# Attention in six whole-kind bundles per pass, and TensorE's queue in source order, from unit 5 on

## The chip, the cores and the metric

The kernel runs on one core of a Trainium2 chip. The metric is device time in microseconds, lower is better: the median of several executions of the whole program. Five engines work side by side, each through its own queue in order: TensorE (PE; its weight loads are listed apart as PEld), VectorE (DVE), ScalarE (ACT), GpSimd (POOL) and SyncE (SP), which here issues nearly all DMA transfers.

## The reference

The program is a gated linear attention with complex decay, followed by a bilinear feed-forward, all in float32.

```python
B, H, S, D = 4, 8, 768, 48
mag = sqrt(a_re**2 + a_im**2); scale = min(mag, 0.999) / (mag + 1e-6)
for t in range(S):                       # state S_re, S_im: [B, H, D, D]
    new_re = ar * S_re - ai * S_im       # ar, ai: the scaled decay of step t
    new_im = ar * S_im + ai * S_re
    S_re, S_im = new_re + outer(k[t], v[t]), new_im
    y[t] = q[t] @ S_re
x = y as [3072, 384]
out = ((x @ w_a) * (x @ w_b)) @ w_out    # w_a, w_b: [384, 1536], w_out: [1536, 384]
```

## The kernel before, in words

The recurrence is computed in chunks of 128 time steps, the feed-forward for 256 tokens at a time. The unit of work is one chunk of two batch rows, called halves i = 0 and 1 here: 6 chunks times 2 pairs make NU = 12 units of 256 tokens. Units 0 to 5 are the six chunks of the first pair, 6 to 11 those of the second, so units 0 and 6 are first chunks (no state comes in) and units 5 and 11 last ones (no state goes out).

A unit goes through three stages.

*Preparation* (`prep` and `scale`, VectorE and ScalarE): running products of the complex decay over the chunk, and their product with q and k, into the tile `qk`. Ten DMA transfers on SyncE's queue (`stack`) then lay `qk` out anew as `stk`, one column block for each head. `qk` and `stk` exist once each: the transfers wait until TensorE has read the old `stk`, and the next `qk` load stands behind them in the queue.

*Attention* (`attn`, mostly TensorE), for each half i: **scores** (8 matmuls, two PSUM tiles "pm" of four heads; VectorE masks each into a tile "am"), **transposes** of the scaled k (8, into two "pm" tiles; ScalarE copies them to "kt"), **outputs** (masked scores times v plus, except in a first chunk, the incoming state times q, in four column tiles of the array, into "xp"; ScalarE copies this to "xh" and VectorE puts the rounding residual, the piece **residual**, into "xl"), and **state** (8 matmuls into two "pm" tiles; VectorE adds them to the state tile "u"). Scores, transposes and state are given out in two groups hg of four heads, outputs in two halves. Full float32 matmuls appear as two records each in the profile. The pool of "pm" has two buffers, "am" and "kt" have two each, "xp" has one.

*Feed-forward* (`gemm1` and `gemm2`): a pass over twelve blocks f0 to f11 of the hidden dimension. The first GEMM of a block is 18 matmuls into "ab" (hi and lo parts of x and the weights, so that a fast float format reaches float32 accuracy); ScalarE and VectorE form the product of the two halves and split it into "hh" and "hl"; the second GEMM, 6 matmuls, follows LAG = 2 blocks later.

The main loop runs pass w of the feed-forward on unit w, and inside it the attention of unit w + 1 and the preparation of units w + 2 and w + 3. What is given out where is written in that loop: `attn` is a generator that issues one piece at each step, and `slot()` takes steps from it, twice in each block, from block ATTN_AT = 6 on; at block STACK_AT = 10 it is drained. So in passes 4 and later, block f6 has its pieces one after the first GEMM and one after the second. These orders are only proposals: a list scheduler builds the queue of each engine from priorities (source order, brought forward for instructions inside `tc.high_priority`) and from its own estimate of when operands are ready. It does so once, when the program is built; on the chip each queue then runs in that fixed order.

The order of attention pieces before, for all units but the first, is the list `order`:

```python
order = [(scores, 0, 0), (scores, 0, 1), (transposes, 0, 0), (transposes, 0, 1),
         (outputs, 0, 0), (outputs, 0, 1), (scores, 1, 0), (residual, 0, 0), (state, 0, 0), (scores, 1, 1),
         (state, 0, 1), (transposes, 1, 0), (transposes, 1, 1), (outputs, 1, 0),
         (outputs, 1, 1), (state, 1, 0), (residual, 1, 0), (state, 1, 1)]
```

Lines that are named later: scores L385, mask L388, transposes L396, their copy L400, outputs L425, copy to xh L429, residual L434, state L442, its addition L449, first GEMM L486, its product and split L494 to L497, second GEMM L504, qk load L340, stack L352; in the preparation L292, L297, L300, L306, L322 to L328.

Of the kernel before, what the change touches and what calls it, by code (L numbers as in the profile page):

```python
# [20 lines left out]
NCH = S // C  # L21
# [25 lines left out]
EARLY = 2  # L47
WARM = 8
HB = 3
O_BUFS = 3  # L50
CONV_ON_AB = 7
NCHK = NU * G + NU + 1
# [6 lines left out]
STACK_AT = (11, 11, 11, 10, 10)  # L59
# [11 lines left out]
def tile_kernel(ctx: ExitStack, tc: tile.TileContext, a_d, qk_d, v_d, w_d, qn_d, kn_d, vn_d, an_d, out_d):  # L71
    nc = tc.nc
    vec, act, pe, sync = nc.vector, nc.scalar, nc.tensor, nc.sync
# [57 lines left out]
    def split_weights():  # L131
        for f in range(NF):
            for m, (c0, n) in enumerate(WPART):
                raw = raws[f, m]
                t = moe.tile([128, n], F32, name="o_sb", bufs=O_BUFS)
                tu = t.bitcast(U32)
# [202 lines left out]
    def load_qk(u):  # L339
        sync.dma_start(out=qk[:, :, 1, 0:2 * TOK], in_=qk_d[u])  # L340

    def stack(u, cols=None):
        n = RUN if rescaled(u % NCH) else 2 * TOK
        if cols is None:
            cols = slice(TOK if u < EARLY else 0, n)
        for h in range(H):
            r0 = h * D
            while r0 < (h + 1) * D:
                j, p = divmod(r0, 128)
                m = min((h + 1) * D - r0, 128 - p)  # L350
                d0 = 2 * (r0 - h * D)
                sync.dma_start(out=stk[d0:d0 + 2 * m, h, cols], in_=qk[p:p + m, j, :, cols])  # L352
                r0 += m
# [4 lines left out]
    def load_v(u):  # L358
        for i in range(2):
            t = vpool.tile([128, 512], F32, name="v_t")  # L360
            sync.dma_start(out=t, in_=v_d[u, i])
            v_tiles[u, i] = t
# [8 lines left out]
    def attn(u, xh, xl):  # L371

        c = u % NCH
        last = c + 1 == NCH
# [61 lines left out]
        def state(i, hg):  # L436
# [10 lines left out]
            with tc.high_priority(offset=ATTN_FIRST):  # L447
# [4 lines left out]
                if rescaled(c):  # L452
                    vec.tensor_tensor(out=uv, in0=uv, in1=sv, op=ALU.mult)
# [5 lines that stand above are left out]
        if u == 0:  # L459
            order = [(scores, 0, 0), (scores, 0, 1), (outputs, 0, 0), (outputs, 0, 1), (scores, 1, 0), (scores, 1, 1),  # L460
                     (residual, 0, 0), (outputs, 1, 0), (outputs, 1, 1), (transposes, 0, 0), (transposes, 0, 1),
                     (residual, 1, 0), (state, 0, 0), (state, 0, 1), (transposes, 1, 0), (transposes, 1, 1),
                     (state, 1, 0), (state, 1, 1)]
        for fn, i, g in order:
            if not (last and fn in (transposes, state)):
                fn(i, g)
                yield

    def pieces(u):
        return 12 if u % NCH + 1 == NCH else 18  # L470

    def new_x():
        return (moe.tile([128, NJ, TOK], F32, name="xh"), moe.tile([128, NJ, TOK], F32, name="xl"))
# [6 lines left out]
    def gemm1(f, xh, xl, ps_ab=ps_ab, moe=moe):  # L480
        ab = ps_ab.tile([128, 512], F32, name="ab")
        for m in range(2):
            n = 0
            for i in range(NJ):
                for part, xt in ((0, xh), (0, xl), (1, xh)):
                    pe.matmul(out=ab[:, m * TOK:(m + 1) * TOK],  # L486
                              lhsT=r(w_ab(f, part, m * NJ + i)),
                              rhs=r(xt[:, i, :]), start=n == 0, stop=n == 8)
                    n += 1
        h_t = moe.tile([128, TOK], F32, name="h_t")  # L490
        hh = moe.tile([128, TOK], F32, name="hh", bufs=HB)
        hl = moe.tile([128, TOK], F32, name="hl", bufs=HB)
        with tc.high_priority(offset=MOE_FIRST):
            act.copy(out=h_t, in_=ab[:, 0:TOK])  # L494
            vec.tensor_tensor(out=h_t, in0=ab[:, TOK:2 * TOK], in1=h_t, op=ALU.mult)  # L495
            act.copy(out=r(hh), in_=h_t)  # L496
            vec.tensor_tensor(out=r(hl), in0=h_t, in1=hh, op=ALU.subtract)  # L497
        return hh, hl

    def gemm2(f, hh, hl, os_):  # L500
        for tt in range(2):
            ts = slice(tt * 128, (tt + 1) * 128)
            for n, (ht, part) in enumerate(((hh, 0), (hh, 1), (hl, 0))):
                pe.matmul(out=os_[tt][:, 0:DM], lhsT=r(ht[:, ts]), rhs=r(w_t[f, 2][:, part, :]),  # L504
                          start=(f == 0 and n == 0), stop=(f == NF - 1 and n == 2))
# [107 lines left out]
    def drain(gen, ns=None):  # L613
        if gen is None:
            return
        left = ns
        for cost in gen:
            if left is not None:
                left -= cost or 0
                if left <= 0:  # L620
                    return
# [10 lines left out]
    for _ in attn(0, *x_cur):  # L632
        drain(p1, P1_A)
    pend = []

    def second():
        w2, f2, hh, hl, os2 = pend.pop(0)
        gemm2(f2, hh, hl, os2)
        if f2 == NF - 1:
            for tt in range(2):  # L640
                o_sb = moe.tile([128, DM], F32, name="o_sb", bufs=O_BUFS)
                with tc.high_priority(offset=MOE_FIRST):
                    act.copy(out=o_sb, in_=os2[tt][:, 0:DM])
                act.dma_start(out=out_d[w2, tt], in_=o_sb)

    pgen = None
    for w in range(NU):
        last = w + 1 == NU
        x_nxt = None if last else new_x()
        at = None if last else attn(w + 1, *x_nxt)  # L650
        if not last:
            load_v(w + 1)
        os_ = [ps_o.tile([128, 512], F32, name=f"o{t}") for t in range(2)]
        slots = [0, 2 * (STACK_AT[min(w, 4)] + 1 - max(ATTN_AT[min(w, 4)], 0 if w else P1_AT + 1))]
        left = [pieces(w + 1)]

        def slot():
            if at is None or f < ATTN_AT[min(w, 4)] or (w == 0 and f <= P1_AT) or not slots[1]:
                return
            n = -(-left[0] // slots[1])  # L660
            slots[1] -= 1
            for _ in range(n):
                next(at, None)
                left[0] -= 1

        for f in range(NF):
            if w == 0:
                next(ws, None)
                drain(p1, P1_F)
                if f == P1_AT:  # L670
                    drain(p1)
                    stack(1)
                    for i in range(WARM):
                        wp = ps_m.tile([128, 512], F32, name="pm")
                        pe.matmul(out=wp[:, 0:TOK], lhsT=ident, rhs=qk[:, i % NJ, 1 - i // NJ % 2, TOK:2 * TOK],
                                  start=True, stop=True)
                    load_qk(2)
                    pgen = prep(2)
            pend.append((w, f, *gemm1(f, *x_cur), os_))
            slot()  # L680
            if len(pend) > LAG:
                second()
            slot()
            if f == STACK_AT[min(w, 4)]:
                drain(at)
                if w + 2 < NU:
                    drain(pgen)
                    stack(w + 2)
                if w + 3 < NU:
                    load_qk(w + 3)  # L690
                    pgen = prep(w + 3)
            if w > 0:
                drain(pgen, 2400)
        x_cur = x_nxt
# [8 lines left out]
    vec.tensor_scalar(out=bad, in0=tot[0:1, 0:1], scalar1=128.0 * NCHK, scalar2=None, op0=ALU.not_equal)  # L703
    while pend:
        second()
    fast.close()
    with tc.If(nc.values_load(bad[0:1, 0:1], min_val=0, max_val=1) > 0):
        token_by_token()
# [55 lines left out]
```

## Time and profile before

| | |
|---|---|
| median of 3 runs | 699.11 us (698.85 to 699.16) |
| the profiled execution | 698.89 us, span 697.2 us |
| TensorE busy | 655.2 us, 94% |
| its weight loads | 610.8 us, 88% |
| VectorE busy | 551.8 us, 79% |
| ScalarE busy | 308.9 us, 44% |

Busy time is the union of an engine's instructions. Matmuls overlap in the array and their ends are modelled, so the time that a group of matmuls costs TensorE is read from its start to the start of the next group. A line of the timeline has start, length, engine, source line, operation, output and inputs, shape and count, and in brackets how long the engine stood idle just before and what ended that. A row of the table of stretches has the stretch, its length, the busy time and the number of instructions of PE, PEld, DVE, ACT and POOL, the granted clock of TensorE, the share of DMA time and the DMA rate.

### The profile page before, as it was taken

What the parts mean: (1) busy time and instruction counts of PE and PEld (TensorE: products, weight loads), DVE (VectorE), ACT (ScalarE), POOL (GpSimd) and SP (SyncE); (2) the same over time, 40 slices, a digit from 0 to 9 for tenths busy, and PEclk for the clock granted to TensorE, in tenths of its full rate; (3) what the DMA queues carried; (4) which work ended last, traced back from release to release, by engine and by line L of the source; (5) the groups of instructions that cost most, each with busy time, mean ns of one, the idle gap of its engine ahead of it and who ended that gap; (6) DMA issues with size and microseconds to landing.
All of it is one profiled execution on the core that took longest, in us unless ns stands there. A gap on an engine that the chain in (4) does not pass through costs nothing.

```text
span 697.2 us, 14316 instructions
## 1 busy us (share of the span) xinstructions
PE 655.2 (94%) x5854; PEld 610.8 (88%) x5854; DVE 551.8 (79%) x1241; ACT 308.9 (44%) x618; POOL 5.6 (1%) x11
## 2 busy tenths in 40 slices
PE   3557999999999999999999999999999999999996
PEld 1224889899899999999999999999999999999996
DVE  5999899988888889989899898999989853232221
ACT  6357755634535445245363554535542332221221
POOL 3000000000000000000000000000000000000000
PEclk9567999999999999999999999999999999999999
DMA  8973202411414205134151340511510500400000
GB/s 312 402 291 108 79 1 54 129 55 55 128 42 130 81 28 149 60 98 129 25 160 46 102 134 1 169 67 47 145 46 2 165 25 17 106 24 2 24 1 28
DMA packets 32088, 63.94 MB, mean 92 GB/s; under 512 B 3984, under 2 KB 10640, under 8 KB 32016
## 3 DMA queue, kind: packets, MB, share of 16 engines
q1 hardware_dynamic: 28560, 58.23, 27.0%
q10 hardware_dynamic: 3456, 4.72, 1.9%
q8 instruction: 48, 0.79, 0.5%
q14 instruction: 24, 0.20, 0.1%
HBM read 39.32 MB, written 4.72 MB: 63 GB/s over the span
## 4 chain that ended last, share of the span: by engine, by line
PE 64%; DVE 27%; ACT 4%; DMA 2%; issue 1%; SPq 1%; ACTq 0%; DVEq 0%
PE ab L486 30%; PE o L504 14%; PE xp L425 6%; PE pm L385 5%; PE pm L442 4%; DVE a_t L292 3%; DVE pr L230 2%; DVE qk L312 2%; DVE h_t L495 2%; PE pm L396 2%; DVE hl L497 2%; PE pm L150 2%; DVE z L297 2%; DVE pb L260 1%; DVE z L236 1%
## 5 line engine op out<-in xcount | busy, mean ns | idle before, releaser
L486 PE MATMUL ab<-xh,w 128*128 128x256 f32 x1728 | 339.0, 285 | 0.0
L486 PEld LDWEIGHTS ab<-xh,w 128*128 128x128 f32 x1728 | 278.1, 190 | 1.8 <-issue 1.4
L486 PE MATMUL ab<-xl,w 128*128 128x256 f32 x864 | 245.1, 284 | 0.0
L486 PEld LDWEIGHTS ab<-xl,w 128*128 128x128 f32 x864 | 164.4, 190 | 0.5 <-issue 0.2
L504 PE MATMUL o<-w,hh 128*128 128x384 f32 x576 | 152.3, 344 | 0.0
L494 ACT COPY h_t<-ab 128x256 f32<-128x256 f32 x144 | 53.1, 369 | 176.9 <-PE ab L486 176.8
L495 DVE TENSOR_TENSOR h_t<-ab,h_t 128x256 f32<-128x256 f32 x144 | 60.5, 420 | 72.5 <-ACT h_t L494 72.3
L504 PEld LDWEIGHTS o<-w,hh 128*128 128x128 f32 x576 | 96.8, 190 | 3.7 <-issue 3.0
L504 PE MATMUL o<-w,hl 128*128 128x384 f32 x288 | 96.9, 336 | 0.0
L496 ACT CAST hh<-h_t 128x256 fp32r<-128x256 f32 x144 | 58.0, 403 | 81.1 <-DVE h_t L495 80.9
L497 DVE TENSOR_TENSOR hl<-h_t,hh 128x256 fp32r<-128x256 f32 x144 | 60.5, 420 | 17.5 <-ACT hh L496 17.3
L150 PE MATMUL ab<-o_sb,ident 128*128 128x384 f32 x42 | 29.1, 794 | 29.9 <-DVE o_sb L141 29.8
L385 PE MATMUL pm<-stk 128*128 128x128 f32 x384 | 54.4, 279 | 2.7 <-DMA stk<-qk 2.7
L504 PEld LDWEIGHTS o<-w,hl 128*128 128x128 f32 x288 | 54.1, 188 | 0.0
L385 PEld LDWEIGHTS pm<-stk 128*128 128x128 f32 x384 | 48.7, 191 | 5.9 <-issue 4.8
L230 DVE TENSOR_TENSOR pr<-z 128x384 f32<-128x384 f32 (+1 forms) x91 | 47.1, 524 | 2.4 <-ACT z L216 0.8
L150 PEld LDWEIGHTS ab<-o_sb,ident 128*128 128x128 f32 x42 | 10.2, 286 | 39.8 <-DVE o_sb L141 29.4
L292 DVE TENSOR_TENSOR a_t<-z,b_t 128x768 f32<-128x768 f32 x48 | 44.6, 952 | 0.1
L425 PE MATMUL xp<-am,v_t 128*32 128x128 f32 x768 | 42.5, 277 | 1.3 <-DVE am L388 1.2
L312 DVE TENSOR_TENSOR qk<-qk,z 128x1536 f32<-128x1536 f32 (+1 forms) x28 | 42.7, 1524 | 0.1
L388 DVE TENSOR_TENSOR am<-pm,mask 128x512 f32<-128x512 f32 x48 | 32.8, 685 | 5.0 <-PE pm L385 4.8
L425 PE MATMUL xp<-stk,u 128*32 128x128 f32 x640 | 34.4, 273 | 0.0
(106 smaller groups left out, 761.7 us busy)
## 6 DMA issues: line engine op xcount, KB each, us to landing
w<-in_dram SPq DMA_DIRECT2D x36, 384.0 KB, 8.1
qk<-in_dram SPq DMA_DIRECT2D x12, 768.0 KB, 4.8
a_t<-in_dram SPq DMA_DIRECT2D x11, 768.0 KB, 4.3
stk<-qk SPq DMA_DIRECT2D x42, 192.0 KB, 3.3
v_t<-in_dram SPq DMA_DIRECT2D x24, 256.0 KB, 2.7
out_dram<-o_sb ACTq DMA_DIRECT2D x24, 192.0 KB, 1.9
stk<-qk SPq DMA_DIRECT2D x18, 192.8 KB, 3.4
stk<-qk SPq DMA_DIRECT2D x14, 128.0 KB, 3.1
```

The lines of the kernel that those rows point to most:

```text
L150: pe.matmul(out=lp[:, 0:n], lhsT=ident, rhs=t, start=True, stop=False)
L230: vec.tensor_tensor(out=pr[:, :, :, o:o + n], in0=view(zz, W + at_(i) + 2 * o, [[W, 2], [-W, 2], [2, n]]), in1=tok(slice(1, 3), i - 1, o, ...
L292: vec.tensor_tensor(out=pz[:, s].rearrange("p (j b e) -> p j b e", j=SUB // 2, e=2), in0=zb[:, 1 + s], in1=view(bb, (1 + k - s) * NB, [[0, ...
L312: vec.tensor_tensor(out=qk4[:, :, k, x0:x1], in0=qk4[:, :, 1, x0:x1], in1=z[:, k].rearrange("p (j t) -> p j t", j=NJ).unsqueeze(2).broadca ...
L385: pe.matmul(out=sp[:, h4], lhsT=stk[:, h, ks], rhs=stk[:, h, qs], start=True, stop=True)
L425: pe.matmul(out=xp[qd * 32:(qd + 1) * 32, ti], lhsT=l, rhs=rr, start=st, stop=sp_, tile_position=(0, qd * 32), skip_group_check=True)
L486: pe.matmul(out=ab[:, m * TOK:(m + 1) * TOK], lhsT=r(w_ab(f, part, m * NJ + i)), rhs=r(xt[:, i, :]), start=n == 0, stop=n == 8)
L494: act.copy(out=h_t, in_=ab[:, 0:TOK])
L495: vec.tensor_tensor(out=h_t, in0=ab[:, TOK:2 * TOK], in1=h_t, op=ALU.mult)
L496: act.copy(out=r(hh), in_=h_t)
L497: vec.tensor_tensor(out=r(hl), in0=h_t, in1=hh, op=ALU.subtract)
L504: pe.matmul(out=os_[tt][:, 0:DM], lhsT=r(ht[:, ts]), rhs=r(w_t[f, 2][:, part, :]), start=(f == 0 and n == 0), stop=(f == NF - 1 and n == 2))
```

## The change

From unit 5 on (`LED = 5`, so in passes 4 to 10) the attention has another order and is given out in another way, and TensorE's queue is no longer made by the scheduler.

- The new list puts pieces of one kind together, and `None` marks the end of a bundle. `attn` yields only there; a bundle left empty (in last chunks, which have no transposes and no state) gives no step. A unit has six bundles, a last chunk three.
- `slot(True)`, called after the second GEMM of a block, gives out one bundle in each block listed in `led_f`: f5 to f10, or f6, f8 and f10 for a last chunk. The call between the GEMMs does nothing there.
- `tc.manual_schedule` for TensorE, entered at the start of pass 4 and left after the last second GEMM: from there on TensorE's instructions stand in its queue as the source issues them. The other engines' queues are still made by the scheduler, from the new source order.

```diff
+LED = 5
...
+        if u >= LED:
+            order = [(scores, 0, 0), (scores, 0, 1), None, (transposes, 0, 0), (transposes, 0, 1), None,
+                     (outputs, 0, 0), (outputs, 0, 1), (scores, 1, 0), (scores, 1, 1), (residual, 0, 0), None,
+                     (state, 0, 0), (state, 0, 1), None, (transposes, 1, 0), (transposes, 1, 1), None,
+                     (outputs, 1, 0), (outputs, 1, 1), (residual, 1, 0), (state, 1, 0), (state, 1, 1), None]
-        for fn, i, g in order:
-            if not (last and fn in (transposes, state)):
-                fn(i, g)
-                yield
+        given = 0
+        for piece in order:
+            if piece is None:
+                if given:
+                    yield
+                given = 0
+            elif not (last and piece[0] in (transposes, state)):
+                piece[0](*piece[1:])
+                given += 1
+                if u < LED:
+                    yield
 
     def pieces(u):
+        if u >= LED:
+            return 3 if u % NCH + 1 == NCH else 6
         return 12 if u % NCH + 1 == NCH else 18
...
+    ordered = ExitStack()
...
+        led_f = [STACK_AT[4] - 6 // left[0] * k for k in range(left[0])] if w + 1 >= LED else None
+        if w + 1 == LED:
+            ordered.enter_context(tc.manual_schedule(engines={pe.engine}))
+
+        def slot(end=False):
+            if led_f is not None:
+                if end and f in led_f and at is not None:
+                    next(at, None)
+                return
...
             if len(pend) > LAG:
                 second()
-            slot()
+            slot(True)
...
     while pend:
         second()
+    ordered.close()
```

The lines of `attn` move down by one, those of `gemm1` and `gemm2` by 15. The queues of the built programs show what moved. First TensorE in block f6 of pass 7, before: between two first GEMMs ("ab") stand the scores ("pm<-stk"), a second GEMM ("o"), and the transposes ("pm<-ident,stk").

```order
L486 MATMUL ab<-xh,w_757 128x256
L385 MATMUL pm<-stk 128x128 x8
L504 MATMUL o_5466<-w_482,hh 128x384 x2
L504 MATMUL o_5466<-w_482,hl 128x384
L504 MATMUL o_5467<-w_482,hh 128x384 x2
L504 MATMUL o_5467<-w_482,hl 128x384
L396 MATMUL pm<-ident,stk 128x96 x8
L486 MATMUL ab<-xh,w_827 128x256
```

The same two kinds with the change, in blocks f5 and f6 of pass 7:

```order
L519 MATMUL o_5469<-w_452,hl 128x384
L386 MATMUL pm<-stk 128x128 x8
L501 MATMUL ab<-xh,w_747 128x256
...
L519 MATMUL o_5468<-w_482,hh 128x384 x2
L519 MATMUL o_5468<-w_482,hl 128x384
L519 MATMUL o_5469<-w_482,hh 128x384 x2
L519 MATMUL o_5469<-w_482,hl 128x384
L397 MATMUL pm<-ident,stk 128x96 x8
L501 MATMUL ab<-xh,w_827 128x256
```

The scores stand one block earlier, behind the second GEMM, and a whole first GEMM and a second one lie between them and the transposes, which refill the same two "pm" buffers.

Second, VectorE at the same place, before: the mask (L388) stands behind the operations L302 to L306 of the preparation, and in the block after them.

```order
L495 TENSOR_TENSOR h_t<-ab,h_t 128x256
L297 TENSOR_TENSOR z<-a_t 128x768
L497 TENSOR_TENSOR hl<-h_t,hh 128x256
L302 TENSOR_TENSOR b_t<-b_5587,rho 128x12
L305 RECIPROCAL rc<-rho 128x6
L331 COPY qk<-rc 128x3x2 x2
L306 TENSOR_TENSOR a_t<-a_t 128x768
L495 TENSOR_TENSOR h_t<-ab,h_t 128x256
L388 TENSOR_TENSOR am<-pm,mask 128x512 x2
L497 TENSOR_TENSOR hl<-h_t,hh 128x256
```

With the change:

```order
L510 TENSOR_TENSOR h_t<-ab,h_t 128x256
L298 TENSOR_TENSOR z<-a_t 128x768
L512 TENSOR_TENSOR hl<-h_t,hh 128x256
L389 TENSOR_TENSOR am<-pm,mask 128x512 x2
L303 TENSOR_TENSOR b_t<-b_5589,rho 128x12
L306 RECIPROCAL rc<-rho 128x6
L307 TENSOR_TENSOR a_t<-a_t 128x768
L332 COPY qk<-rc 128x3x2 x2
L510 TENSOR_TENSOR h_t<-ab,h_t 128x256
```

Both masks stand behind "hl" of block f5, ahead of those preparation operations.

Third, the end of the attention in TensorE's queue, before (pass 7, blocks f9 to f10):

```order
L504 MATMUL o_5467<-w_847,hl 128x384
L425 MATMUL xp<-am,v_t 32x128 x4
L425 MATMUL xp<-stk,u_112 32x128 x4
...
L442 MATMUL pm<-v_t,kt 96x48 x4
L486 MATMUL ab<-xh,w_1011 128x256
```

and with the change (block f10 into f11):

```order
L519 MATMUL o_5469<-w_905,hl 128x384
L426 MATMUL xp<-am,v_t 32x128 x4
L426 MATMUL xp<-stk,u_112 32x128 x4
...
L443 MATMUL pm<-v_t,kt 96x48 x8
L501 MATMUL ab<-xh,w_1100 128x256
```

The last outputs have moved from block f9 to block f10, and both state groups follow them at once; before, one of them followed, and the other came after f10.

More of the change, by code (lines that the diff above doesn't have):

```diff
@@ L655, in tile_kernel @@
         left = [pieces(w + 1)]
-        def slot():
+        led_f = [STACK_AT[4] - 6 // left[0] * k for k in range(left[0])] if w + 1 >= LED else None
[6 more added lines that the diff above has]
+                return
             if at is None or f < ATTN_AT[min(w, 4)] or (w == 0 and f <= P1_AT) or not slots[1]:
```

## The prediction

> **What bounds the kernel now.** I read the head of the page first, then a table of stretches cut at the first feed-forward matmul of each pass, then TensorE's timeline inside one pass. "Pass w" is the feed-forward of unit w, twelve blocks f0 to f11; the attention of unit w + 1 is given out inside it, so "from unit 5 on" means passes 4 to 10.
>
> ```profile
> span 697.2 us, 14316 instructions
> PE 655.2 (94%) x5854; PEld 610.8 (88%) x5854; DVE 551.8 (79%) x1241; ACT 308.9 (44%) x618; POOL 5.6 (1%) x11
> ...
> 303.70:350.78 47.08, 46.80 (x450) 45.30 (x449) 43.30 (x89) 21.11 (x41) 0.00 (x0) 1.00 0.30 88
> 350.78:399.72 48.94, 48.94 (x433) 47.69 (x433) 45.53 (x95) 24.98 (x51) 0.00 (x0) 1.00 0.35 104
> 399.72:450.96 51.24, 50.86 (x497) 49.41 (x497) 46.43 (x103) 27.30 (x51) 0.00 (x0) 1.00 0.38 107
> 450.96:502.34 51.38, 50.99 (x497) 49.37 (x497) 48.94 (x108) 24.82 (x49) 0.00 (x0) 1.00 0.27 82
> 502.34:553.25 50.91, 50.78 (x497) 49.44 (x497) 47.03 (x117) 16.55 (x36) 0.00 (x0) 1.00 0.23 66
> 553.25:603.81 50.56, 50.56 (x498) 49.41 (x497) 22.84 (x45) 15.77 (x35) 0.00 (x0) 1.00 0.23 67
> 603.81:650.21 46.40, 46.40 (x449) 45.17 (x449) 13.66 (x31) 10.98 (x28) 0.00 (x0) 1.00 0.03 10
> ...
> 553.25:572.42 19.17, 19.17 (x146) 19.17 (x145) 13.00 (x23) 8.42 (x17) 0.00 (x0) 1.00 0.18 63
> ```
>
> The seven rows are passes 4 to 10: stretch, length, then busy time of TensorE, its weight loads, VectorE, ScalarE and GpSimd, and the granted clock, 1.00 throughout. By its busy time TensorE is idle for less than 0.4 us in any pass (matmuls' ends are modelled, which covers some short waits), so it sets the end, and a pass gets shorter only if TensorE's queue does. VectorE is close behind (48.94 of 51.38 us in pass 7) until pass 9, where it needs only 22.84. The last row is blocks f0 to f5 of pass 9, with no attention in them: 3.195 us a block, so a bare pass is 38.34 us. What is left over is attention: 12.22 us in pass 9, 8.06 in pass 10 (a last chunk, without transposes and state). Passes 6, 7 and 8 hold exactly the work of pass 9, yet last 0.68, 0.82 and 0.35 us longer; pass 4 holds that of pass 10 and lasts 0.68 longer. Those differences are waits; the rest is work and the seams between kinds of matmul. The change can touch both.
>
> **The change, part by part.** Passes 0 to 3 and blocks f0 to f4 of every pass stand in TensorE's queue as they did. In a middle pass the attention stood in nine places between feed-forward matmuls; now it stands in six, each after the second GEMM of blocks f5 to f10: scores of half 0; transposes of half 0; outputs of half 0 with scores of half 1; state of half 0; transposes of half 1; outputs and state of half 1. In passes 4 and 10 six places become three. No instruction is added or removed.
>
> *Seams.* TensorE in pass 9, without waits (time from one start to the next is what a run costs):
>
> ```profile
> 572.43 0.28 PE L486 MATMUL ab<-xh,w 128*128 128x256 f32 x1
> ...
> 574.57 1.95 PE L385 MATMUL pm<-stk 128*128 128x128 f32 x16
> 576.27 0.59 PE L504 MATMUL o<-w,hh 128*128 128x384 f32 x2
> ...
> 577.40 0.82 PE L396 MATMUL pm<-ident,stk 96*128 96x96 f32 x8
> 578.01 0.36 PE L486 MATMUL ab<-xh,w 128*128 128x256 f32 x1
> ...
> 580.33 0.43 PE L425 MATMUL xp<-am,v_t 128*32 128x128 f32 x8
> ...
> 582.21 0.62 PE L504 MATMUL o<-w,hh 128*128 128x384 f32 x2
> ...
> 583.39 1.05 PE L385 MATMUL pm<-stk 128*128 128x128 f32 x8
> 584.20 0.36 PE L486 MATMUL ab<-xh,w 128*128 128x256 f32 x1
> ...
> 595.94 0.88 PE L442 MATMUL pm<-v_t,kt 128*96 128x48 f32 x8
> 596.64 0.36 PE L486 MATMUL ab<-xh,w 128*128 128x256 f32 x1
> ...
> 598.87 0.52 PE L504 MATMUL o<-w,hh 128*128 128x384 f32 x2
> ...
> 599.91 0.80 PE L442 MATMUL pm<-v_t,kt 128*96 128x48 f32 x8
> 600.53 0.37 PE L486 MATMUL ab<-xh,w 128*128 128x256 f32 x1
> ...
> 602.77 0.51 PE L504 MATMUL o<-w,hh 128*128 128x384 f32 x2
> ```
>
> A bare first GEMM takes 2.14 us (572.43 to 574.57), a bare second 1.04 (598.87 to 599.91). After scores the second takes 1.13, after state the first takes 2.23 or 2.24: leaving scores or state costs 0.09. Between transposes and outputs the first GEMM takes 2.32, 0.18 over: 0.09 to leave transposes and 0.09 to enter the column-tiled outputs. After outputs the second takes 1.18: 0.14 to leave them. Sixteen scores take 1.70 and eight 0.81, so a second eight in a run costs 0.89, 0.08 more than the first. Outputs of one half take 1.88, eight transposes 0.61, eight state matmuls 0.62 alone and 0.70 right after outputs (I take the second eight at 0.70 too). Scores right after outputs do not occur here; an early pass has them:
>
> ```profile
> 186.69 0.71 PE L385 MATMUL pm<-stk 128*128 128x128 f32 x4
> 187.24 0.80 PE L442 MATMUL pm<-v_t,kt 128*96 128x48 f32 x8
> ```
>
> Four in 0.55 us against four eighths of 0.89: 0.10 for the seam, between the 0.08 of outputs to state and the 0.14 of outputs to the second GEMM. The six bundles of a middle pass are then 1.70 + 0.09 = 1.79; 0.61 + 0.09 = 0.70; 0.09 + 1.88 + 0.10 + 1.70 + 0.09 = 3.86; 0.62 + 0.70 + 0.09 = 1.41; 0.70; 0.09 + 1.88 + 0.70 + 0.70 + 0.09 = 3.46. Sum 11.92 against 12.22: 0.30 less. In a last chunk 1.79 + 3.86 + (0.09 + 1.88 + 0.14) = 7.76 against 8.06, again 0.30. Pass 5 (a first chunk, outputs half as long) has the same seams. Seven passes: **2.1 us**.
>
> [...] The rows charge 0.09 for leaving the untiled kinds too, so the sum goes by the rows.
>
> *Waits.* What the longer passes wait for:
>
> ```profile
> 473.98 0.59 PE L504 MATMUL o<-w,hh 128*128 128x384 f32 x2
> ...
> 475.61 1.15 PE L396 MATMUL pm<-ident,stk 96*128 96x96 f32 x8 [0.34 <-DVE am L388]
> ...
> 424.79 0.55 PE L396 MATMUL pm<-ident,stk 96*128 96x96 f32 x4 [0.38 <-DVE am L388]
> ...
> 339.34 0.30 PE L425 MATMUL xp<-am,v_t 128*32 128x128 f32 x1 [0.28 <-DVE am L388]
> ...
> 374.94 0.97 PE L396 MATMUL pm<-ident,stk 96*128 96x96 f32 x8
> ...
> 473.67 0.96 DVE L306 TENSOR_TENSOR a_t<-a_t 128x768 f32<-128x768 f32 x1 [0.77 <-ACT a_t L300]
> 474.54 0.41 DVE L495 TENSOR_TENSOR h_t<-ab,h_t 128x256 f32<-128x256 f32 x1
> 474.88 1.28 DVE L388 TENSOR_TENSOR am<-pm,mask 128x512 f32<-128x512 f32 x2
> ```
>
> The score tiles and the transposes share the two PSUM buffers "pm". In pass 7 the scores end at 473.98 and the transposes stand one second GEMM (1.13 us) behind them, but VectorE is held by preparation for a later unit and masks the scores only until 476.16, 2.2 us after the scores end. TensorE stands for 0.5 us ahead of the transposes (1.63 us from 473.98 against 1.13) and 0.33 inside them (1.15 against 0.82). Pass 6 has the same at 424.79; pass 5 a small one, 0.97 against 0.82; in pass 4 the outputs wait for the mask at 339.34. The waits sum to 0.68 + 0.15 + 0.68 + 0.82 + 0.35 = 2.7 us over passes 4 to 8. In the new order a whole block (3.19 + 0.08 us) lies between a kind and the next user of its buffers, so the same 2.2 us of lateness is covered with 1 us to spare; outputs come two blocks after their scores. I take the old waits as gone: **2.7 us**. If the cover went, the price would be these 2.7 again.
>
> *Moved the other way.* The last outputs of a pass now stand in f10, not f9. Between their end and the next pass, which needs "xh" and "xl" of them at its first two matmuls, lie 1.40 us of state, 0.09, and block f11, 4.7 us, where pass 9 has 7.9 (595.94 to 603.81). The chain outputs, ScalarE copy, VectorE residual:
>
> ```profile
> 597.13 0.54 DVE L434 TENSOR_TENSOR xl<-xp,xh 128x384 fp32r<-128x384 f32 x1
> ...
> 542.80 7.57 SPq L352 DMA_DIRECT2D stk<-qk  x10
> ...
> 553.72 0.61 SPq L340 DMA_DIRECT2D qk<-in_dram  x1
> ...
> 561.56 0.95 DVE L328 TENSOR_TENSOR qk<-qk,a_t 128x768 f32<-128x768 f32 x1
> ...
> qk<-in_dram SPq DMA_DIRECT2D x12, 768.0 KB, 4.8
> ```
>
> The residual ends 1.7 us after the outputs (597.67), with 3.0 us left; it costs nothing unless VectorE is behind by three prep operations of 0.95. The ten "stk" transfers on SyncE's queue overwrite what these outputs read, so they start later: at 542.80 they began 10.5 us ahead of pass 9; now the outputs themselves start only 3.46 - 0.09 + 3.19 = 6.6 us ahead of it, so the transfers come at least 3.9 us later. The scores that need them stand in f5, over 15 us on, and the "qk" load behind them in the queue (553.72 plus its 4.8 us median) lands 9.2 us or more into pass 9, where VectorE's operation on it (561.56, 8.3 us in) would wait 1 to 2 us. The "hl" that is queued behind it is due only two blocks later: nothing on TensorE. I take new waits as 0; their upper bound is the third rival.
>
> *Sum.* 698.89 us is the profiled execution's own time (span 697.2 and 1.7 around it). 698.89 - 2.1 - 2.7 = 694.1; the median of the runs shown lies 0.2 above the profiled one, so **694.2 us** for the median, 0.7% less.
>
> **The rivals.**
>
> *The waits move instead of going.* VectorE runs at up to 95% of a pass, and masks, residuals and state updates now come to it in clusters. If each cluster makes TensorE stand as long as now, only the seams are saved: 699.1 - 2.1 = 697.0. For it: VectorE's order is fixed ahead, and it was up to 2.2 us late. Against: three times the distance on TensorE. A half of it would give 695.6.
>
> [...]
>
> *The end of a pass becomes the wait, slower.* Its place is "xl" ahead of the next pass's first GEMM. It decides from the point where VectorE is 3.0 us late with it: five preparation operations of 0.95 ahead of it would be 4.75 us, a wait of 1.75 in each of the six passes 4 to 9, 10.5 us, less the 4.8 gained: 704.8. Against: in the slowest case, pass 8, VectorE's new order sets three operations of about 0.95 or less between f10's "hl" and the residual; and VectorE keeps some 28 us free in pass 9, so it has no lasting backlog.
>
> That the change does not do what it says is excluded by the order of the built program.
>
> **How the numbers follow.** [...] Faster by over 0.2% is then 0.87. Since nothing but these seams and waits is touched, little can lie below 693; the range goes down to 692.8 for the seams' rounding and up to 697.4, where nearly all waits stay.
>
> **What would show it.** Right: passes 4 to 10 last 46.1, 48.5, four times 50.3, and 46.1 us; no TensorE row of transposes or outputs there is marked as waiting for the mask; scores after outputs cost 0.10 over those alone. Wrong: a wait "<-DVE xl" or "<-ACT xh" at the first matmul of a pass (third rival), or rows of transposes or state waiting for VectorE (first rival), or passes 6 to 8 still longer than pass 9.

## The result, and the profile after

The changed kernel takes **695.0 us** (median of 5 runs, 694.02 to 695.88) against 698.85 (698.4 to 699.16) for the kernel before in the same rounds: a ratio of 0.9946, 95% interval 0.9931 to 0.996. The forecast was 694.2; its range, 693.2 to 695.2, had a chance of 0.62, 694.8 inside it (only the outputs' seams saved, an estimate of the author) 0.08, 695.2 to 697.7 (waits that stay) 0.17, 697.7 to 700.5 (gain and new waits cancelling) 0.06 and slower 0.07. One execution of the kernel before, beside experiments 3, 6 and 7, took 1614.88 us; it is left out of the ratios, and no trace shows its cause. First the head of the page of the changed kernel, its chain of waits by engine, and the group of the second GEMM with the idle time before it:

```profile
span 693.3 us, 14308 instructions
PE 651.4 (94%) x5854; PEld 610.1 (88%) x5854; DVE 552.8 (80%) x1241; ACT 308.3 (44%) x618; POOL 5.6 (1%) x11
...
PE 77%; DVE 15%; ACT 3%; DMA 2%; issue 1%; SPq 0%; ACTq 0%; DVEq 0%
...
L519 PE MATMUL o<-w,hh 128*128 128x384 f32 x576 | 149.8, 340 | 0.7 <-ACT o_sb L658 0.7
```

The same line of the chain on the page of before:

```profile
PE 64%; DVE 27%; ACT 4%; DMA 2%; issue 1%; SPq 1%; ACTq 0%; DVEq 0%
```

The span is 3.9 us shorter, VectorE's share of the chain that ends last falls from 27% to 15%, and one group of TensorE has a releaser that it did not have before: the second GEMM now waits for `o_sb`, ScalarE's copy of the output accumulators. The table of stretches, cut at the first matmul of each pass, passes 4 to 10 (stretch, length, busy PE, PEld, DVE, ACT, POOL, granted clock, DMA share, GB/s):

```profile
303.45:349.52 46.07, 46.07 (x449) 45.17 (x449) 42.50 (x88) 21.09 (x41) 0.00 (x0) 1.00 0.30 89
349.52:398.97 49.45, 48.72 (x433) 47.53 (x433) 45.92 (x96) 24.34 (x51) 0.00 (x0) 1.00 0.33 100
398.97:449.17 50.20, 50.20 (x497) 49.22 (x497) 46.91 (x103) 27.10 (x51) 0.00 (x0) 1.00 0.34 97
449.17:499.38 50.21, 50.21 (x497) 49.23 (x497) 47.93 (x107) 25.43 (x49) 0.00 (x0) 1.00 0.26 80
499.38:549.59 50.21, 50.21 (x497) 49.23 (x497) 46.68 (x117) 16.35 (x36) 0.00 (x0) 1.00 0.22 65
549.59:599.94 50.35, 50.35 (x497) 49.18 (x497) 24.57 (x46) 15.71 (x35) 0.00 (x0) 1.00 0.23 68
599.94:646.01 46.07, 46.07 (x449) 45.17 (x449) 14.07 (x31) 11.08 (x28) 0.00 (x0) 1.00 0.11 31
```

| pass | 4 | 5 | 6 | 7 | 8 | 9 | 10 | sum |
|---|---|---|---|---|---|---|---|---|
| before | 47.08 | 48.94 | 51.24 | 51.38 | 50.91 | 50.56 | 46.40 | 346.51 |
| forecast | 46.1 | 48.5 | 50.3 | 50.3 | 50.3 | 50.3 | 46.1 | 341.9 |
| after | 46.07 | 49.45 | 50.20 | 50.21 | 50.21 | 50.35 | 46.07 | 342.56 |

Six of seven passes came out within 0.1 us of the forecast. Passes 6, 7 and 8 are now alike to 0.01 us, which is what "the waits are gone" looks like: equal work, equal time. **Pass 5 is the exception: it grew by 0.51 us where 0.4 less was expected**, and pass 9, though near its forecast, has 0.15 more than its equals.

*The seams.* TensorE's timeline in pass 9 of the changed kernel, transposes of half 0 and the bundle of outputs and scores (start, length, line, operation; the time from one start to the next is the cost):

```profile
573.88 0.82 PE L397 MATMUL pm<-ident,stk 96*128 96x96 f32 x8
574.49 0.36 PE L501 MATMUL ab<-xh,w 128*128 128x256 f32 x1
...
576.72 0.52 PE L519 MATMUL o<-w,hh 128*128 128x384 f32 x2
...
577.86 0.42 PE L426 MATMUL xp<-am,v_t 128*32 128x128 f32 x8
...
579.75 2.05 PE L386 MATMUL pm<-stk 128*128 128x128 f32 x16
581.55 0.36 PE L501 MATMUL ab<-xh,w 128*128 128x256 f32 x1
...
583.78 0.51 PE L519 MATMUL o<-w,hh 128*128 128x384 f32 x2
```

This gives: transposes 0.61, the first GEMM behind them 2.23; the second GEMM ahead of the outputs 1.14 (0.10 over its bare 1.04); outputs 1.89; scores behind outputs 1.80 against 1.70 alone; the first GEMM behind scores 2.23. The seams in these rows are there at the prices of the prediction, to 0.01, also the one that no middle pass before had shown: outputs to scores, 0.10. What TensorE does at a seam no row tells; measured are 0.10 ahead of the outputs, and 0.09 on the next GEMM behind the scores and behind the transposes.

*The old waits.* The masks of half 0 in pass 7 of the changed kernel, TensorE and then VectorE:

```profile
470.04 0.36 PE L501 MATMUL ab<-xh,w 128*128 128x256 f32 x1
...
473.32 0.82 PE L397 MATMUL pm<-ident,stk 96*128 96x96 f32 x8
```

```profile
471.03 1.29 DVE L389 TENSOR_TENSOR am<-pm,mask 128x512 f32<-128x512 f32 x2
```

The scores end at 470.04, where the next GEMM starts, and VectorE has masked them at 472.32, 2.3 us later: as late as the 2.2 us before. The transposes start 3.3 us behind the scores, so they have 1.0 us to spare. This excludes that the waits went because VectorE became faster or got a better order. The tightest place is half 1 of the same pass: the mask ends 3.1 us after the scores and 0.2 us ahead of the state matmuls.

*The new wait.* TensorE in block f2 of pass 5, changed kernel:

```profile
355.39 0.51 PE L519 MATMUL o<-w,hh 128*128 128x384 f32 x2
355.74 0.33 PE L519 MATMUL o<-w,hl 128*128 128x384 f32 x1
358.95 0.62 PE L519 MATMUL o<-w,hh 128*128 128x384 f32 x2 [0.73 <-ACT o_sb L658]
```

and ScalarE's queue at the same time:

```profile
356.65 1.49 ACT L182 ACTIVATE a_t<-a_t 128x1536 f32<-128x1536 f32 x1
...
358.14 0.39 ACT L511 CAST hh<-h_t 128x256 fp32r<-128x256 f32 x1
358.43 0.85 ACT L658 COPY o_sb<-o 128x384 f32<-128x384 f32 x2
```

The first two rows of TensorE are the last second GEMM of pass 4, the third is the first one of pass 5. The two accumulators "o" exist once. Because the second GEMM runs two blocks late, only one first GEMM (2.14 us) lies between those rows, and in that gap ScalarE has to copy "o" out. It does not, since a 1.49 us square (L182, the scale of unit 8) and a cast stand ahead of the copies in its queue. The same places before, ScalarE and then TensorE:

```profile
356.93 1.49 ACT L181 ACTIVATE a_t<-a_t 128x1536 f32<-128x1536 f32 x1
...
358.71 0.85 ACT L643 COPY o_sb<-o 128x384 f32<-128x384 f32 x2
```

```profile
357.01 0.33 PE L504 MATMUL o<-w,hl 128*128 128x384 f32 x1
359.33 0.52 PE L504 MATMUL o<-w,hh 128*128 128x384 f32 x2
```

The order on ScalarE was the same, and the copies came just in time: 1.7 us after the last matmul into "o" began. Now TensorE comes out of pass 4 1.26 us earlier by this profile (349.52 against 350.78; 0.25 of it is that pass 4 began earlier, 303.45 against 303.70), but the copies only 0.28 earlier (358.43 against 358.71): within the pass, TensorE gained 1.01 and ScalarE next to nothing. What holds ScalarE is VectorE: ahead of the square ScalarE stood idle for 3.19, 1.66 and 0.46 us until VectorE released its rows at 352.24, 354.58 and 355.45. VectorE's long products at the start of pass 5 came 0.28 us earlier too, the changed kernel's first:

```profile
350.12 1.76 DVE L313 TENSOR_TENSOR qk<-qk,z 128x1536 f32<-128x1536 f32 x1
```

```profile
350.40 1.76 DVE L312 TENSOR_TENSOR qk<-qk,z 128x1536 f32<-128x1536 f32 x1
```

So VectorE keeps its own pace there (it was busy for 42.50 of the 46.07 us of pass 4); the 1.0 us that pass 4 gained is given back two blocks into pass 5 (its block f2 lasts 4.19 us instead of 3.21).

### The profile page after: what moved, and what is told of

It reads as the page before. It is cut to its first block, busy times and chain, and to the rows that moved or that the text cites. A ratio compares the mean times of both kernels' runs of the same rounds, so it can differ in the third digit from the quotient of the medians.

```text
span 693.3 us, 14308 instructions
## 1 busy us (share of the span) xinstructions
PE 651.4 (94%) x5854; PEld 610.1 (88%) x5854; DVE 552.8 (80%) x1241; ACT 308.3 (44%) x618; POOL 5.6 (1%) x11
## 4 chain that ended last, share of the span: by engine, by line
PE 77%; DVE 15%; ACT 3%; DMA 2%; issue 1%; SPq 0%; ACTq 0%; DVEq 0%
PE ab L501 37%; PE o L519 18%; PE xp L426 7%; PE pm L386 6%; PE pm L443 4%; DVE qk L313 2%; PE pm L397 2%; PE pm L151 2%; DVE a_t L293 2%; PE ab L151 1%; DVE o_sb L140 1%; DMA stk<-qk 1%; DVE o_sb L142 1%; DVE h_t L510 1%; DVE hl L512 1%
## 5 line engine op out<-in xcount | busy, mean ns | idle before, releaser
L519 PE MATMUL o<-w,hh 128*128 128x384 f32 x576 | 149.8, 340 | 0.7 <-ACT o_sb L658 0.7
```

## The experiments

None of these kernels leaves out any of the computation. The kernel before took 698.8 us (698.1 to 699.73) beside experiments 1, 2, 4 and 5, and 699.25 beside the others.

**1. TensorE's queue in source order, without the bundles.** The kernel before, with its own list and slots:

```diff
+    ordered = ExitStack()
...
+        if w + 1 == LED:
+            ordered.enter_context(tc.manual_schedule(engines={pe.engine}))
...
+    ordered.close()
```

> The kernel before with only the queue half of the change: TensorE's instructions in source order from pass 4 on, the old list of pieces and the old places. The built TensorE queue is that of before but for one place in pass 6. Theory (bundles and their places do all of it): the waits for the mask in passes 4 to 8 stay, 2.3 to 3 us in sum, and so do the seams; 698.9 us, within 0.5 of the kernel before, pass 9 at 50.5 to 50.6 us. Rival (source order is what removes the waits): passes 6 to 8 fall to pass 9's 50.56, about 696.2 us.

Measured: 701.75 us (6 runs), ratio 1.0043 (1.0028 to 1.0058): slower. TensorE's queue is that of the kernel before but for four transposes in pass 6, which the scheduler had put into the middle of a first GEMM. Passes 6 and 8 last 51.79 and 52.73 us where they took 51.24 and 50.91. The two have different causes. In pass 6 it is those four transposes, here with source order and then in the kernel before:

```profile
437.32 0.55 PE L397 MATMUL pm<-ident,stk 96*128 96x96 f32 x4 [0.40 <-DVE am L389]
```

```profile
437.73 0.50 PE L396 MATMUL pm<-ident,stk 96*128 96x96 f32 x4
```

The mask ahead of them came at the same time in both; the scheduler's place inside the GEMM had hidden the wait. In pass 8 TensorE's order is unchanged, but VectorE's and ScalarE's queues, which the scheduler still makes, came out otherwise there. TensorE and VectorE:

```profile
528.84 1.15 PE L397 MATMUL pm<-ident,stk 96*128 96x96 f32 x8 [1.69 <-DVE am L389]
```

```profile
526.10 1.75 DVE L313 TENSOR_TENSOR qk<-qk,z 128x1536 f32<-128x1536 f32 x1
...
528.10 1.28 DVE L389 TENSOR_TENSOR am<-pm,mask 128x512 f32<-128x512 f32 x2
```

The mask now stands behind a 1.75 us product (in the kernel before, both masks stood ahead of it). So source order on TensorE by itself removes no wait, and as long as a mask has only one second GEMM to hide behind, its wait depends on which preparation operation the scheduler puts ahead of it. The forecast, 698.9 within 0.5, took the other queues as unchanged. The counterpart needed no run: built without the manual schedule, the changed kernel has the same queue on all five engines, instruction for instruction. The bundles do everything; the other half of the change does nothing.

**2. The distance taken away.** The changed kernel with the transposes of half 0 in the same bundle as the scores of half 0 (they used to stand one block behind). In passes 5 to 9 all later bundles move up by one block with them:

```diff
-            order = [(scores, 0, 0), (scores, 0, 1), None, (transposes, 0, 0), (transposes, 0, 1), None,
+            order = [None, (scores, 0, 0), (scores, 0, 1), (transposes, 0, 0), (transposes, 0, 1), None,
```

> The changed kernel with the transposes of half 0 in the same bundle as its scores (no feed-forward matmul between them) in passes 5 to 9; the later bundles stand one block earlier. Theory (distance on TensorE is what hides VectorE's lateness): the transposes wait for the mask again, 0.6 us at least (pass 9, VectorE idle) and up to 2 us in each of passes 5 to 8, 4 to 8 us in all, less 0.1 a pass for the seam saved: 698 to 702 us, with transposes rows marked as waiting for the mask. Rival (the waits went because VectorE's own order became better): no waits there, 694.5 to 695.

Measured: 703.97 us (one run). Passes 5 to 9 last 50.36, 52.19, 52.43, 53.69 and 50.88. TensorE in pass 7, scores and transposes, and then VectorE:

```profile
471.21 1.95 PE L386 MATMUL pm<-stk 128*128 128x128 f32 x16
...
474.89 0.30 PE L397 MATMUL pm<-ident,stk 96*128 96x96 f32 x1 [1.74 <-DVE am L389]
```

```profile
472.94 0.96 DVE L307 TENSOR_TENSOR a_t<-a_t 128x768 f32<-128x768 f32 x1 [1.08 <-ACT a_t L301]
...
474.15 1.28 DVE L389 TENSOR_TENSOR am<-pm,mask 128x512 f32<-128x512 f32 x2
```

VectorE is 2.5 us late with the mask here, against 2.3 in the changed kernel; without a block between them TensorE pays for it, in each of passes 5 to 9. The passes are 9.1 us longer in all (259.55 against 250.42), of which 1.5 in pass 8 have another cause, shown at the end; the other 7.6 us are what taking the distance away costs, more than the old waits, since here not even a second GEMM is left in between. Together with the masks' times above: **the old waits went because of the distance, as the prediction said.**

**3. The distance alone.** The kernel before, with two empty steps behind the scores of half 0 in units 6 to 10, so that a block lies between them and the transposes, and nothing else:

```diff
+        def rest(i, _):
+            pass
...
+        if u > 5 and not last:
+            order[2:2] = [(rest, 0, 0)] * 2
...
-        return 12 if u % NCH + 1 == NCH else 18
+        return 12 if u % NCH + 1 == NCH else 20 if u > 5 else 18
```

> The kernel before with two empty steps behind the scores of half 0 in passes 5 to 9, so that the transposes stand a first and a second GEMM behind the scores instead of a second one alone; the nine places of a pass and the scheduler's queue stay. Theory (distance alone removes the old waits, the bundles' seams are the other half): no wait ahead of the transposes of half 0, passes 6 to 8 at 50.5 to 50.6 if nothing else gets too close, pass 4 as before at 47.1: 696.7 to 697.2 us; later pieces come closer to each other, so that a wait of up to 0.7 us a pass may turn up at f8 or f9. Rival (the whole-kind order is needed): the waits at the transposes stay, 698.5 to 699.

Measured: 700.26 us (one run). The waits ahead of the transposes of half 0 are gone: block f6 lasts 4.97 us and f7 5.87 in all of passes 6 to 9. But the later pieces moved closer together, and the wait moved with them. TensorE in pass 6, the scores of half 1:

```profile
437.03 1.16 PE L385 MATMUL pm<-stk 128*128 128x128 f32 x8 [0.79 <-DVE am L388]
```

Passes 5, 6 and 7 last 49.35, 51.61 and 51.62, longer than before; passes 8 and 9 last 50.87 and 50.56, as before. So the waits at the transposes went, as expected, but the wait that turned up behind them, 1.0 us in passes 6 and 7 where up to 0.7 was allowed for, took more than that gain, and the time missed the 696.7 to 697.2 of the theory. A distance at one place shifts the wait to the next user of the two "pm" buffers. The bundles give all of them the distance at once.

**4. A seam put back.** The changed kernel with each bundle of outputs cut in two, the first half after the block's first GEMM, the second after its second:

```diff
-                     (outputs, 0, 0), (outputs, 0, 1), (scores, 1, 0), (scores, 1, 1), (residual, 0, 0), None,
+                     (outputs, 0, 0), None, (outputs, 0, 1), (scores, 1, 0), (scores, 1, 1), (residual, 0, 0), None,
...
-                     (outputs, 1, 0), (outputs, 1, 1), (residual, 1, 0), (state, 1, 0), (state, 1, 1), None]
+                     (outputs, 1, 0), None, (outputs, 1, 1), (residual, 1, 0), (state, 1, 0), (state, 1, 1), None]
...
-                if end and f in led_f and at is not None:
+                if f in (led_f if end else (7, 10) if left[0] == 6 else (8, 10)) and at is not None:
```

> The changed kernel with each outputs bundle cut in its two halves, one given out after the first GEMM of the same block and one after the second: no wait is touched, each pass enters and leaves the column-tiled outputs two more times, fourteen times over seven passes. Theory (seams are paid in full): by the prediction's prices 0.23 each, 3.2 us; by the rows of the kernel before, where two halves apart in pass 10 cost 1.01 each against 1.88 together, up to 0.34 each, 4.7 us: passes 6 to 9 at 50.7 to 50.9 us, 698 to 700 us in all. Rival (seams overlap with neighbouring matmuls and cost nothing in sum): 695.0.

Measured: 698.53 us (one run). Passes 4 and 5 of it:

```profile
303.13:349.89 46.76, 46.76 (x449) 45.17 (x449) 43.16 (x89) 21.21 (x41) 0.00 (x0) 1.00 0.30 88
349.89:399.42 49.53, 49.42 (x433) 47.58 (x433) 45.53 (x95) 24.60 (x51) 0.00 (x0) 1.00 0.33 102
```

Pass 4 is 0.69 longer (46.76 against 46.07), as are passes 6 to 8 and 10: 0.345 for each cut. Pass 5 is only 0.08 longer, for its block f2 fell from 4.19 to 3.59 us: when TensorE comes out of pass 4 later, the wait for `o_sb` shrinks by nearly as much. This shows from the other side that this wait gives back what pass 4 gains.

**5. The squares behind the copies.** The changed kernel with the squares of unit 8's scale queued behind pass 4's copies on ScalarE; the rest of that scale is given out later with them:

```diff
+    o_copies = {}
...
-            act.activation(out=t, in_=a_t[:, :, hs], func=AF.Square, accum_out=sums[:, u + n:u + n + 1])
+            with tc.issue_after(o_copies[4]) if u == 8 else ExitStack():
+                act.activation(out=t, in_=a_t[:, :, hs], func=AF.Square, accum_out=sums[:, u + n:u + n + 1])
...
-            yield 880 + (next(sg, 0) if i > 1 else 0)
+            yield 880 + (next(sg, 0) if i > (SUB if u == 7 else 1) else 0)
...
-                    act.copy(out=o_sb, in_=os2[tt][:, 0:DM])
+                    o_copies[w2] = act.copy(out=o_sb, in_=os2[tt][:, 0:DM]).ins
```

> The changed kernel with one instruction of ScalarE moved: in pass 5 the 1.49 us squares of unit 8's preparation are queued behind the copies that empty the two output accumulators of pass 4. Theory (the new wait of 1.0 us in pass 5, ahead of the second GEMM of f0, comes from ScalarE's queue holding those copies back): pass 5 falls from 49.45 to 48.4 to 48.6 us and the whole by 0.9 to 1.0: 694.0 to 694.2. Rival (VectorE sets the pace of passes 4 and 5 together, and what pass 4 gained is lost in pass 5 whatever ScalarE does): another wait of about 1 us appears in pass 5 or 6, time unchanged at 695.0.

Measured: 694.2 us (5 runs), ratio 0.9938 (0.9924 to 0.9952). Passes 5 and 9:

```profile
348.85:397.30 48.45, 48.45 (x433) 47.47 (x433) 45.18 (x94) 23.43 (x50) 0.00 (x0) 1.00 0.34 102
...
547.94:598.90 50.96, 50.48 (x497) 49.19 (x497) 25.18 (x48) 15.72 (x35) 0.00 (x0) 1.00 0.23 65
```

Pass 5 is now 48.45, the 48.5 of the forecast: the squares ahead of the copies were the cause there. But pass 9 grew from 50.35 to 50.96, by the same kind of wait. ScalarE, then TensorE:

```profile
555.60 0.48 ACT L660 COPY o_sb<-o 128x384 f32<-128x384 f32 x1
555.97 0.95 ACT L311 ACTIVATE a_t<-a_t,biases 128x768 f32<-128x768 f32 x1
...
557.11 0.49 ACT L660 COPY o_sb<-o 128x384 f32<-128x384 f32 x1
```

```profile
557.64 0.62 PE L521 MATMUL o<-w,hh 128*128 128x384 f32 x2 [0.48 <-ACT o_sb L660]
```

An exponential (L311) stands between the two copies. It stood there in the changed kernel too, where the wait was 0.15 us:

```profile
557.02 0.95 ACT L309 ACTIVATE a_t<-a_t,biases 128x768 f32<-128x768 f32 x1
...
558.15 0.49 ACT L658 COPY o_sb<-o 128x384 f32<-128x384 f32 x1
```

The queues of ScalarE and VectorE have the same order in both kernels from pass 6 on. What changed is that TensorE enters pass 9 1.65 us earlier and the second copy comes only 1.04 us earlier. So 0.6 of the 1.0 us won in pass 5 was given back in pass 9, as the rival had it in kind, though not in passes 5 or 6: the seven passes take 342.2 us against 342.56, and that the median hit the forecast of 694.0 to 694.2 is in part the spread of runs.

**6. All copies ahead, beside the changed kernel once more.** Experiment 5, with the copies of passes 5 and later at a higher priority and one exponential behind pass 8's copies:

```diff
-        act.activation(out=a_t[:, 1], in_=a_t[:, 1], func=AF.Exp, scale=-1.0, bias=b_inv)
+        with tc.issue_after(o_copies[8]) if u == 11 else ExitStack():
+            act.activation(out=a_t[:, 1], in_=a_t[:, 1], func=AF.Exp, scale=-1.0, bias=b_inv)
...
-                with tc.high_priority(offset=MOE_FIRST):
+                with tc.high_priority(offset=2 * MOE_FIRST if w2 >= LED - 1 else MOE_FIRST):
```

> The changed kernel with the copies that empty the output accumulators put ahead of preparation work in ScalarE's queue, in pass 5 (squares of unit 8 behind them) and in pass 9 (an exponential of unit 11 behind them), and ahead in priority in passes 5 to 11. Theory: both waits at the second GEMM of f0 go, pass 5 at 48.45, pass 9 at 50.2, the other passes as in the changed kernel (46.07, 50.21, 50.21, 50.21, 46.07): 1.0 to 1.2 us less than the changed kernel, 693.6 to 694.0. Rival (passes 4 to 9 are paced by VectorE and the wait wanders): as before this fix, pass 9 or another takes 0.6 to 1.0 us, 694.2 to 694.8.

> The changed kernel itself, on the same chip as the one with the copies first: 694.5 to 695.5 us.

Measured: 694.09 us (693.64 to 694.3, 5 runs), ratio to the kernel before 0.9928 (0.9914 to 0.9942); the unedited changed kernel on the same chip 694.73 (694.19 to 695.71, 4 runs), ratio 0.9937 (0.9921 to 0.9953), with the same pass lengths as in its first profile to 0.03 us, the wait in pass 5 among them. By the whole time the two can hardly be told apart. By the passes they can: 48.44, 50.36 and 50.28 us for passes 5, 7 and 9 (pass 7 has a new 0.15, pass 9 still 0.08), and 341.68 for the seven against 342.56. This is the fastest kernel of the study; some 0.9 of the 1.15 us of new waits were to be had back.

**7. One unit earlier.** The changed kernel with `LED = 4`, which bundles the attention in pass 3 too:

```diff
-LED = 5
+LED = 4
```

> The changed kernel with the change one unit earlier, from unit 4 on: the scores stand in f5 of pass 3, where the stk transfers land only 3 to 4 us later (in the kernel before they land 0.1 us into f7, after a wait of 1.9 us inside f6). Theory (the transfers are what forbids an earlier start, and from pass 4 on they have the lead that the prediction counts on): pass 3 waits for the transfers, 51.0 grows to 53 to 55 us, pass 5 loses its new wait of 1.0 because VectorE gains the same time: 696 to 698 us. Rival (no such limit): pass 3 falls to 50.2, 694.2.

Measured: 700.9 us (one run). Pass 3 lasts 56.61 us instead of 50.99. TensorE there, the first of four such rows:

```profile
273.92 1.06 PE L386 MATMUL pm<-stk 128*128 128x128 f32 x4 [0.76 <-DMA stk<-qk]
```

The scores of the first bundle want `stk` in f5, and the ten transfers into it begin, in that pass, only at 267.95, some 15 us into the pass; those of pass 9 in the changed kernel begin 5.9 us ahead of it. The direction was right; the size, 5.6 us, was more than the 2 to 4 expected. Block f5, with the waits, lasts 8.66 us instead of 4.90. The excess over the forecast is in block f6, behind the waits, which lasts 6.43 us instead of 3.88 without any wait, at a mean granted clock of 0.55:

```profile
277.55:283.98 6.43, 6.43 (x34) 6.39 (x34) 5.69 (x11) 2.05 (x5) 0.00 (x0) 0.55 0.37 122
```

The wait in pass 5 shrank to 0.1 us, as expected, but waits of 0.8 and 0.5 us turned up in passes 8 and 9: passes 4 to 10 take 342.9 us, no less than in the changed kernel.

## Why the prediction came out as it did

**Seams: right, slightly small.** 0.30 us a pass were forecast; the passes without waits before show 50.56 to 50.2 and 46.40 to 46.07, 0.33 to 0.36. Over seven passes that is 2.4 us against 2.1; 0.05 a pass is what rounding a dozen rows to 0.01 can make. A smaller sum, an estimate of the author, prices only the outputs' seams: 0.09 + 0.14 a visit by the rows of before, one visit less a pass, 1.6 us over seven. It is right about where the gain comes from; that the other seams cost nothing no run shows. The untiled kinds do charge 0.09, by the 2.23 us of the first GEMM behind scores and behind transposes. But putting them together saves next to nothing, because a second eight scores in a run cost 0.08 more than the first. What is saved is the one visit to the outputs that each of the seven passes has less (two instead of three): experiment 4 prices a visit at 0.345 us, which is the whole gain of a pass. That sum came to 1.6 us only because a visit was priced at 0.23, without the 0.14 by which two halves apart (1.01 each) cost more than 1.88 together.

**Old waits gone: right, cause confirmed.** No row of transposes, scores or outputs in passes 4 to 10 waits for the mask any more, and passes 6 to 8 equal each other, so the 2.7 us were had in full. The masks are as late as before and the distance covers them; experiment 2 brings the waits back by taking the distance away, experiment 1 keeps them with the order of the queue alone, experiment 3 shows that a distance at one place is not enough. The "1 us to spare" was right for half 0; for half 1 of pass 7 0.2 us were left.

**"I take new waits as 0": this step failed.** The wait is 1.0 us in pass 5 and 0.15 in pass 9; 698.89 - 2.4 - 2.7 + 1.15 gives 694.9, where 695.0 was measured. That the total missed by only 0.8 us is in part luck: the seams, 0.3 more than forecast, hid some of the 1.15. The prediction asked what VectorE delivers to the matmuls of the attention and to the start of a pass ("xl"), and did not ask what ScalarE delivers at the end of one. The copies of "o" had no slack already before (the second GEMM of f0 began 0.62 us after the start of the two copies, 0.85 us long together), and VectorE and with it ScalarE did not follow TensorE 1 us forward. Experiment 5 shows the same once more: with the wait in pass 5 removed, most of the gain stuck at the copies of pass 9. The general form of the first rival, waits that move instead of going, was right for a fifth of the gain, but at a place that it did not name. Passes 6 to 8 have no such wait: there no operation over 0.95 us stands just ahead of the copies or between them in ScalarE's queue. An operation of 0.95 us between them cost 0.15 us in pass 9 and none in pass 6, so the length alone does not decide; it is how late ScalarE comes to them.

**The third rival, a wait at the end of a pass, fell.** "xl" is ready at 597.02 in pass 9 (its row starts at 596.48 and takes 0.54), 2.9 us ahead of pass 10; 3.0 had been worked out. Nothing waits there in any pass.

**The transfers moved as said.** The ten into `stk` begin at 543.73, 5.9 us ahead of pass 9 where it was 10.5: 4.6 later (at least 3.9 forecast). The `qk` load follows at 554.67, VectorE's operation on it starts 10.8 us into the pass instead of 8.3, and no TensorE row in passes 4 to 10 waits for either. Experiment 7 shows what it costs when that lead is not there.

What stays open: the changed kernel's median came out at 695.0 once and 694.73 once, so of the 0.8 us between forecast and result a part is within the spread of runs; the wait of 1.15 us is in both profiles.

## What to carry to other kernels

When small buffers are shared between kinds of work on an in-order engine, put a whole block of other work between one user and the next, for all users at once: in experiment 3 a distance at one place only passed the wait on. When the bounding engine gets faster in one stage, list everything that other engines must finish before the next stage, each with its slack in the old trace, evacuation copies of single-buffered accumulators first; an engine that is near full there (VectorE, busy for 42.50 of the 46.07 us of pass 4) may not move forward with it, and then the gain is returned at the next place without slack, as in passes 5 and 9 here. Where a scheduler makes the queues, compare all queues after a change to one of them: in experiment 1 a change at one place of TensorE's queue in pass 6 went with 1.8 us more in pass 8, through VectorE's.

## What the runs showed of the hardware that was not expected

Cutting one visit of the column-tiled outputs in two costs 0.345 us, more than the 0.23 of entering and leaving them that the rows of before add up to; the halves themselves take 1.01 us each against 1.89 for the whole.

In experiment 2 TensorE stood for 1.5 us in pass 8, and behind that its granted clock fell to 0.50. (In experiment 7 it fell behind four waits of 0.2 to 0.8 us, to a mean of 0.55 over the 6.43 us of the block behind them.) The table of stretches, to the end of that wait, the block behind it, and one microsecond of it:

```profile
520.40:527.99 7.59, 6.04 (x50) 5.67 (x49) 7.59 (x11) 1.51 (x4) 0.00 (x0) 1.00 0.00 0
527.99:536.56 8.57, 8.57 (x107) 8.12 (x106) 7.14 (x15) 2.64 (x6) 0.00 (x0) 0.80 0.01 2
...
529.00:530.00 1.00, 1.00 (x7) 1.00 (x6) 0.84 (x2) 0.49 (x1) 0.00 (x0) 0.50 0.00 0
```

The block lasts 8.57 us where it takes 7.06 or 7.07 in passes 6, 7 and 9: 1.5 us more, as long as the wait itself. By these clocks the low one lasted some 3.4 us (0.50 in three whole microseconds, 0.86 and 0.94 in those beside them). What sets it off no run shows: waits of 1.74 us in pass 7 of the same run and of 1.69 in experiment 1 left the clock at 1.00.
